# Two MLP weight loads moved ahead of a token load, and a later landing assumed by the scheduler, in a linear-attention plus MLP block

## The chip, the cores and the metric

One core of one Trainium2 chip. The metric is the device time in microseconds of one execution, lower is better. Runs of a single-core program are compared in rounds: the two kernels alternate on the same chip, and a ratio is the mean time of one kernel's fast runs over that of the other's of the same rounds, so it is not quite the ratio of the medians quoted. The granted clock is the share of TensorE's full clock that the chip allowed.

Names used below: TensorE is the matmul engine (PE in the profile, its weight loads PEld), VectorE is DVE, ScalarE is ACT, GpSimd is POOL, SP is the engine whose queue issues nearly all loads here. A load lands when all of its data are there.

## The reference

The block adds three things, for 2048 tokens of width 640, all in bfloat16:

```python
xn = layernorm(x)
# attention, 32 heads of 20: feature maps of q and k are two softmaxes each
q, k, v = split(xn @ wqkv)
phi_q = concat(softmax(q @ w_phi), softmax(-q @ w_phi))      # 40 features per head
phi_k = concat(softmax(k @ w_phi), softmax(-k @ w_phi))
kv, z = sum_s phi_k v, sum_s phi_k
o = (phi_q @ kv) / (phi_q @ z + 1e-6)
# MLP with 1536 hidden columns
h = silu(xn @ w1) * (xn @ w3)
out = x + o @ wo + h @ w2
```

## The kernel before

The program is written as small steps (a matmul group, a softmax, a load), each a stream's next item. At build time a list scheduler estimates when each step could start, takes the earliest, and so fixes the order of instructions on every engine; on the chip each engine runs its list in order and waits on semaphores. The scheduler's estimate of a load:

```python
            if o.dma:
                turn = "T" == o.part                       # a transposing load
                ...
                self.bus = max(self.bus, t + 0.5) + o.cost / rate
                o.end = self.bus + (2.3 if turn and t > 80 else 1.6 if turn else 1.3 if t < 4.5 else 1.9)
```

These constants change no computing instruction and no load. They only move steps in the order (and with it two semaphore instructions of TensorE: 46 in the profile before, 44 after).

The loads that are issued at once, all but one of them from SP, in this order:

```python
    def w13(a, b):                                          # two MLP weights, columns a to b: 640 KB each for 512
        P.dma("SP", w1_s[:, :, a:b], w1_t[:, :, a:b])
        P.dma("SP", w3_s[:, :, a:b], w3_t[:, :, a:b])
    def first_loads():
        ...                                                 # tokens 0-3, wv
        w13(0, 512)
        P.dma("SP", phi_s[:], phi_t)
        P.dma("SP", wqkT[:, DC:2 * DC, :], A_wqkv[:, D:2 * D], True)     # key weights, transposed
        load_x(4, 8)                                        # token tiles 4-7, 640 KB
        load_x(8, 12)
        w13(512, 1024)
```

One MLP step is ten matmuls of 512 columns, five with `w1` and then five with `w3`; steps 0 to 3 use weight columns 0 to 511 and step 4 is the first to need columns 512 to 1023. In the second half, each token tile's query features are computed (`Wqp`), normalised, transposed by a DMA into `EqT`, and used by eleven small matmuls (`KVc,EqT`) that belong to no fixed place in the order: the scheduler fits MLP steps and output tiles between.

```python
    def warm_up():                                          # before the first data has come
        for n, rep in ((4, 8), (1, 7)):                     # 8 matmuls of 512 columns, 7 of 128
            for _ in range(rep):
                mm(bank(7, 128 * n), zero[:], zero[:]..., True, True, ...)
```

The softmax here doesn't subtract the row's maximum and nothing guards it: scores larger than these inputs give would overflow.

Of the kernel before, what the change touches and what calls it, by code (L numbers as in the profile page):

```python
# [45 lines left out]
class _Program:  # L46
# [123 lines left out]
    def commit(self, ops):  # L170
        for o in ops:
            o.idx = len(self.ops)
            o.deps = self.find_deps(o)
            t = self.free[o.eng]
            for d in o.deps:
                t = max(t, d.end + 0.07)
            o.start = t
            if o.dma:
                turn = "T" == o.part
                self.free[o.eng] = t + (max(1.28, o.cost / 120e3) if turn else 0.46)  # L180
                rate = (280e3 if o.cost < 300e3 else 235e3) if turn else 270e3 if t < 2.9 else 330e3 if t < 4.5 else 345e3 if t < 20 else 285e3
                self.bus = max(self.bus, t + 0.5) + o.cost / rate
                o.end = self.bus + (2.3 if turn and t > 80 else 1.6 if turn else 1.3 if t < 4.5 else 1.9)
            else:
                o.end = t + o.cost + LATENCY[o.eng]
                self.free[o.eng] = t + o.cost - OVERLAP[o.eng]
            self.ops.append(o)
            if o.eng == "POOL" and not o.dma:
                self.pool = o
            for g in o.reads:  # L190
                if isinstance(g, tuple):
                    self.bank.setdefault(g, {})[o.eng] = o
                else:
                    self.last_r.setdefault(g, {})[("dma", o.idx) if o.dma else o.eng] = o
            for g in o.writes:
                if isinstance(g, tuple):
                    self.bank.setdefault(g, {})[o.eng] = o
                else:
                    self.last_w[g] = o
                    self.last_r.pop(g, None)  # L200
# [45 lines left out]
def bass_parallel_sum__linear_kernel_hedgehog__glu_gated_swiglu__prompt_kernel(  # L246
# [160 lines left out]
    def w13(a, b):  # L407
        P.dma("SP", w1_s[:, :, a:b], w1_t[:, :, a:b])
        P.dma("SP", w3_s[:, :, a:b], w3_t[:, :, a:b])

    def load_x(a, b):
        P.dma("SP", x_tok[:, a:b, :], x_t[:, a:b, :])

    def first_loads():
        load_x(0, 1)
        o = P.dma("ACT", x_tok[:, 1:2, :], x_t[:, 1:2, :])
        o.reads = P.regions(zero[:])
        load_x(2, 3)
        for a, b in ((0, 2), (2, 4), (4, DC)):
            P.dma("SP", wv[:, a:b, :], wqkv_t[:, a:b, 2 * D:3 * D])  # L420
        load_x(3, 4)
        w13(0, 512)
        P.dma("SP", phi_s[:], phi_t)
        P.dma("SP", wqkT[:, DC:2 * DC, :], A_wqkv[:, D:2 * D], True)
        load_x(4, 8)
        load_x(8, 12)
        w13(512, 1024)


    def consts():  # L430
# [269 lines left out]

    def norms():
        yield lambda: (memset("DVE", zero[:], 0.0), memset("DVE", warm[:], 0.0), first_loads(), consts())
        yield lambda: act_sums(1)
        yield lambda: ln_stats(0, 1)
# [280 lines left out]
```

## Time and profile before

268.77 us, median of three runs (268.58 to 268.81); the profiled execution has a span of 266.6 us.

TensorE is the bound.

The chain of waits of the kernel before, in order of time (start us, length us, what):

```profile
14.78 9.38 DMA w_s<-in_B_w_dram
24.15 0.14 issue
24.29 101.68 PE PS L104 x839
125.97 0.04 issue
126.00 138.34 PE PS L104 x968
```

The chain is TensorE's own work but for two breaks: it starts from a weight load that landed at 24.15 us, and it breaks once more near 126 us. The waits view names the two releasers (us in total, times, longest):

```profile
PEld PS L104 <- DMA EqT<-eqt: 0.4, 1, 0.4
PE PS L104 <- DMA w_s<-in_B_w_dram: 0.4, 1, 0.4
```

TensorE's timeline of the kernel before (start us, us, engine, line, operation, output<-inputs, count, idle before it and its releaser):

```profile
12.76 4.48 PE L104 MATMUL PS<-xnT,w_s 128*128 128x512 bf16 x20
...
22.66 1.24 PE L104 MATMUL PS<-xnT,w_s 128*128 128x512 bf16 x5
24.29 1.24 PE L104 MATMUL PS<-xnT,w_s 128*128 128x512 bf16 x5 [0.39 <-DMA w_s<-in_B_w_dram]
...
27.84 4.24 PE L104 MATMUL PS<-Wkp,xnT 128*128 128x320 bf16 x30
...
122.54 3.42 PE L104 MATMUL PS<-w_s,hT 128*128 128x320 bf16 x24
126.00 0.49 PE L104 MATMUL PS<-KVc,EqT 128*128 128x63 bf16 x11
```

Reading it: matmul ends are modelled, so the 0.39 understates the wait. Five matmuls of 512 columns follow each other every 0.216 us, so the ones that start at 22.66 hand over at 23.74; the next start at 24.29 is 0.55 us late. In the same way the 24 matmuls of 320 columns, 0.136 us apart, that start at 122.54 hand over at 125.80; the start at 126.00 is 0.20 us late. The landings in the trace, in the order of issue: tiles 4-7 at 17.58, tiles 8-11 at 19.37, first weight at 22.43, second weight at 24.16.

### The profile page before, as it was taken

The numbers are of one execution on the slowest core, as the hardware profiler recorded it, in microseconds if no ns is written. First come the engines' busy times: TensorE is split into PE (matmuls) and PEld (weight loads), VectorE is DVE, ScalarE is ACT, GpSimd is POOL, SyncE is SP. The second block draws the span as 40 slices with busy tenths as digits, with TensorE's granted clock in tenths as the row PEclk, the third lists the DMA queues.
The fourth block names the chain that finished last, engine by engine and source line by source line (L and its number), as shares of the span: only waits on it lengthen the run. The fifth ranks groups of instructions, "written<-read, shape, count | busy, mean of one in ns | idle before, by whom it ended". The sixth has DMA issues, their size and how long they took to land.

```text
span 266.6 us, 4819 instructions
## 1 busy us (share of the span) xinstructions
PE 262.1 (98%) x1951; PEld 162.1 (61%) x1951; DVE 182.9 (69%) x312; ACT 107.4 (40%) x227; POOL 95.6 (36%) x107
## 2 busy tenths in 40 slices
PE   7999999999999999999999999999999999999996
PEld 3754666766766756556465655466565746777773
DVE  4567899999777497778767677969775857212112
ACT  5546688898871325332251314451414220000000
POOL 4211289898999032522207030617030430000000
PEclk9999999999999999999999999999999999999999
DMA  7996045962400773619503543061825074331211
GB/s 223 277 316 173 1 105 108 324 85 49 125 0 2 188 247 72 131 28 130 128 0 70 114 85 69 10 128 35 148 52 128 0 126 84 76 98 49 87 38 49
DMA packets 62742, 27.73 MB, mean 104 GB/s; under 512 B 49920, under 2 KB 62720, under 8 KB 62720
## 3 DMA queue, kind: packets, MB, share of 16 engines
q1 hardware_dynamic: 62576, 27.26, 44.4%
q8 instruction: 15, 0.25, 0.4%
q10 hardware_dynamic: 144, 0.16, 0.2%
q14 instruction: 7, 0.06, 0.1%
HBM read 12.81 MB, written 2.62 MB: 58 GB/s over the span
## 4 chain that ended last, share of the span: by engine, by line
PE 90%; SPq 5%; DMA 4%; issue 0%; DVE 0%
PE PS L104 90%; SPq L116 5%; DMA w_s<-in_B_w_dram 4%; DVE xres L104 0%
## 5 line engine op out<-in xcount | busy, mean ns | idle before, releaser
L104 PE MATMUL PS<-xnT,w_s 128*128 128x512 bf16 x480 | 108.6, 379 | 0.4 <-DMA w_s<-in_B_w_dram 0.4
L104 PEld LDWEIGHTS PS<-xnT,w_s 128*128 128x128 bf16 x480 | 46.2, 98 | 51.3 <-DVE Wkp L104 0.9
L104 POOL TENSOR_TENSOR eqt<-eqt,rS 128x600 bf16<-128x600 bf16 (+1 forms) x32 | 41.0, 1304 | 90.8 <-DVE rS L104 90.8
L104 ACT ACTIVATE th<-PS 128x512 f32<-128x512 f32 x48 | 28.6, 595 | 74.0 <-PE PS L104 73.9
L104 PE MATMUL PS<-w_s,hT 128*128 128x320 bf16 (+2 forms) x384 | 54.9, 299 | 0.0
L104 DVE SCALAR_TENSOR_TENSOR t<-th,PS 128x512 bf16<-128x512 f32 x48 | 32.5, 677 | 31.6 <-ACT th L104 31.5
L104 PEld LDWEIGHTS PS<-w_s,hT 128*128 128x128 bf16 x384 | 37.1, 98 | 15.1
L104 POOL TENSOR_TENSOR ekt<-ekt,rS 128x640 bf16<-128x640 bf16 x32 | 39.7, 1273 | 3.9 <-DVE rS L104 3.9
L104 ACT ACTIVATE eqt<-PS 128x240 bf16<-128x240 f32 (+1 forms) x96 | 27.2, 348 | 26.0 <-PE PS L104 24.1
L104 DVE TENSOR_TENSOR xres<-PS,xres 128x640 bf16<-128x640 f32 (+2 forms) x17 | 13.3, 782 | 34.6 <-PE PS L104 34.6
L104 DVE SCALAR_TENSOR_TENSOR hT<-t,PS 128x512 bf16<-128x512 bf16 x48 | 33.0, 687 | 2.0 <-PE PS L104 0.4
L104 ACT ACTIVATE ekt<-PS 128x640 bf16<-128x640 f32 x32 | 22.3, 703 | 7.0 <-PE PS L104 6.4
L104 DVE TENSOR_REDUCE S<-ekt 128x64 f32<-128x1280 bf16 x16 | 23.2, 1452 | 2.2 <-ACT ekt L104 2.2
L104 PE MATMUL PS<-wo_s,oT 128*128 128x320 bf16 (+2 forms) x160 | 24.5, 299 | 0.0
L104 PE MATMUL PS<-wv,xnT 128*128 128x320 bf16 x160 | 24.4, 299 | 0.1
L104 PE MATMUL PS<-Wqp,xnT 128*128 128x360 bf16 (+1 forms) x160 | 24.3, 299 | 0.0
L104 DVE TENSOR_REDUCE S<-eqt 128x66 f32<-128x1320 bf16 x16 | 24.2, 1513 | 0.0
L104 PE MATMUL PS<-Wkp,xnT 128*128 128x320 bf16 x160 | 23.9, 299 | 0.0
L104 PEld LDWEIGHTS PS<-Wqp,xnT 128*128 128x128 bf16 x160 | 15.2, 98 | 7.6
L104 PEld LDWEIGHTS PS<-wv,xnT 128*128 128x128 bf16 x160 | 15.4, 98 | 6.4 <-ACT xnT L104 0.3
L104 PEld LDWEIGHTS PS<-Wkp,xnT 128*128 128x128 bf16 x160 | 15.4, 98 | 6.1
L104 PEld LDWEIGHTS PS<-wo_s,oT 128*128 128x128 bf16 x160 | 15.3, 98 | 6.0
(52 smaller groups left out, 156.7 us busy)
## 6 DMA issues: line engine op xcount, KB each, us to landing
w_s<-in_B_w_dram SPq DMA_DIRECT2D x6, 640.0 KB, 7.2
xres<-in_A_x_dram SPq DMA_DIRECT2D x16, 160.0 KB, 2.5
out_dram<-xres SPq DMA_DIRECT2D x15, 160.0 KB, 1.8
x_tok<-in_A_x_dram SPq DMA_DIRECT2D x3, 640.0 KB, 4.5
w_s<-in_B_w_dram SPq DMA_DIRECT2D x1, 1920.0 KB, 8.8
wo_s<-in_A_wo_dram SPq DMA_DIRECT2D x1, 800.0 KB, 4.7
wv<-in_A_wqkv_dram SPq DMA_DIRECT2D x2, 320.0 KB, 4.3
x_tok<-in_A_x_dram SPq DMA_DIRECT2D x3, 160.0 KB, 2.6
```

The source lines that it names most:

```text
L104: o = _Op(eng, lambda: m(*args, **kw), r, w, cost)
L116: o = _Op(eng, lambda: m(out, in_), self.regions(in_), self.regions(out), nbytes, True)
```

## The change

The intent: bring the weight that TensorE waits for ahead of tokens that are needed 10 us later, and make the scheduler leave more room between the transposing loads of query features and their use.

```diff
-                o.end = self.bus + (2.3 if turn and t > 80 else 1.6 if turn else 1.3 if t < 4.5 else 1.9)
+                o.end = self.bus + (2.7 if turn and t > 80 else 1.6 if turn else 1.3 if t < 4.5 else 1.9)
@@ first_loads
         load_x(4, 8)
+        w13(512, 1024)
         load_x(8, 12)
-        w13(512, 1024)
```

The built programs were compared too. TensorE's order is unchanged up to its matmuls at about 134 us; ACT's and POOL's orders are unchanged throughout.

## The prediction

> **What bounds the kernel now.** TensorE issues without a gap from about 7 us to its end. The page gives PE 98% busy, but matmul ends are modelled, so I used starts: 512-column matmuls follow each other every 0.216 us. The Trainium skill, "TensorE: Matmul & The Clock Gate", "Step-by-step: what each phase is for", gives about 216 ns for N=512; the trace agrees, at a granted clock of 1.00. After 7 us only two places exceed column time by over 0.06 us:
>
> - 24.29 us: 0.55 us (0.4 in the timeline, modelled ends hiding the rest), ended by the second MLP weight load. Landings: token tiles 8-11 19.37, first weight (columns 512-1023) 22.43, second 24.16. The five matmuls before start at 22.66 and need 1.08, so it was due at 23.74.
> - 126.0 us: 0.20 us (0.4 in the waits view), ended by the transposing load of query features of tile 4, which took 5.2 us against a median of 3.7.
>
> The chain of waits agrees: PE 90%, broken at 24.15 and 125.97 alone. Removable from TensorE is therefore about 0.75 us.
>
> **What the change does.**
> 1. Two 640 KB weight loads go ahead of the 640 KB token load on one queue. The skill, "DMA: Bandwidth & Descriptors", "Queues, rings and completion order", says each DMA engine consumes descriptors in ring order; here landings follow issue order. My estimate from those landings: each weight lands 1.8 us sooner, the second near 22.3, 1.4 us before it is due, so the whole 0.55 us goes. The next bound there (the Wkp copy, done at 23.92, for matmuls due after 25.1) isn't met. The tokens land near 24.2; the statistics that read tile 8 start at 34.9, so 10 us of slack remain.
> 2. The assumed landing (2.3 to 2.7) only feeds the scheduler; nothing is added or removed. The built order is unchanged on TensorE up to about 134 us and everywhere on ACT and POOL; TensorE, DVE and SP differ after. The load that now costs 0.20 us is used before that point, behind the same TensorE work, so I expect that wait to stay (0 to 0.4 us). Later loads keep about 0.3 us of slack or more, as before (smallest: 0.26 tile 14, 0.63 tile 11); tile 15 gains some. Worth: 0 ± 0.2 us.
>
> **On the critical path:** all of the 0.55 us. DVE is nearly full (29.3 of 30 us in the 30-60 stretch), but its run of work starts from matmuls that move with TensorE, and so do the later loads. Small slacks near 56 us (transposed tokens 0.39, query weights 0.73) could give back 0.1 if those loads don't move.
>
> **Prediction: 268.2 us** (268.77 - 0.55), 8 in 10 between 267.9 and 268.7. Chances: faster by over 2% 0.01, within 2% 0.98, slower 0.01.
>
> **What would show it.** Right: no PE wait near 24 us; second weight landing near 22.3; the chain no longer through a weight load; about 0.2 us of wait left near 125.5. Wrong for step 1: a weight later than 23.7, or a wait of like size at 56 us. Wrong for step 2: the 125.5 us wait gone, or new waits for query features after 134 us.
>
> **What would make it wrong.** A transposing load that meets other traffic takes 4.7 to 5.2 us (tiles 4, 11, 14) instead of 3.7; in the new order other tiles may be the slow ones, costing up to 1 us each. Or new waits cancel the gain.

## More of the kernel before

The head, part 3 and part 4 of the page of the kernel before: busy time and share by engine, DMA queues (packets, MB, share of 16 engines), and the chain that ended last:

```profile
span 266.6 us, 4819 instructions
PE 262.1 (98%) x1951; PEld 162.1 (61%) x1951; DVE 182.9 (69%) x312; ACT 107.4 (40%) x227; POOL 95.6 (36%) x107
...
q1 hardware_dynamic: 62576, 27.26, 44.4%
q8 instruction: 15, 0.25, 0.4%
...
PE 90%; SPq 5%; DMA 4%; issue 0%; DVE 0%
```

## The result

The changed kernel: 267.92 us median (267.85 to 268.04, six runs), before 268.79 (268.2 to 269.0, six runs); ratio 0.9972, 95% interval 0.9959 to 0.9984. It is correct. By the 2% rule this is "same", with a small gain clear of noise.

The page of the changed kernel:

```profile
span 266.3 us, 4817 instructions
PE 262.7 (99%) x1951; PEld 162.6 (61%) x1951; DVE 182.7 (69%) x312; ACT 107.5 (40%) x227; POOL 95.8 (36%) x107
...
PE 97%; DMA 1%; DVE 1%; POOL 0%; issue 0%; ACT 0%
```

Its chain of waits, from where TensorE takes it over for good:

```profile
10.61 114.99 PE PS L104 x928
125.59 0.03 issue
125.62 138.34 PE PS L104 x968
```

Its waits on loads, and TensorE's timeline at the same places as before:

```profile
PEld PS L104 <- DMA EqT<-eqt: 0.4, 1, 0.4
```

```profile
12.93 4.48 PE L104 MATMUL PS<-xnT,w_s 128*128 128x512 bf16 x20
...
22.82 2.32 PE L104 MATMUL PS<-xnT,w_s 128*128 128x512 bf16 x10
...
27.46 4.24 PE L104 MATMUL PS<-Wkp,xnT 128*128 128x320 bf16 x30
...
122.17 3.42 PE L104 MATMUL PS<-w_s,hT 128*128 128x320 bf16 x24
125.62 0.48 PE L104 MATMUL PS<-KVc,EqT 128*128 128x63 bf16 x11
```

The weight load is out of the chain, the MLP step's ten matmuls run in one piece, and the wait near 126 us is still there (0.19 us by the starts). The landings: first weight 19.53, second weight 22.61, tokens 8-11 24.29. So far this is what was predicted. Two things don't add up, though. The profiled spans differ by 0.4 us only (266.64 and 266.26), since in the changed kernel's profile the first MLP matmul happened to start 0.17 us later; and the timed runs differ by more, 0.87 us by the medians. A wait of 0.55 us read in one execution is not obviously the thing measured.

### The profile page after: what moved, and what is told of

It reads as the page before. It is cut to its first block, busy times and chain, and to the rows that moved or that the text cites. A ratio compares the mean times of both kernels' runs of the same rounds, so it can differ in the third digit from the quotient of the medians.

```text
span 266.3 us, 4817 instructions
## 1 busy us (share of the span) xinstructions
PE 262.7 (99%) x1951; PEld 162.6 (61%) x1951; DVE 182.7 (69%) x312; ACT 107.5 (40%) x227; POOL 95.8 (36%) x107
## 4 chain that ended last, share of the span: by engine, by line
PE 97%; DMA 1%; DVE 1%; POOL 0%; issue 0%; ACT 0%
PE PS L104 97%; DMA x_tok<-in_A_x_dram 1%; DVE bst L104 0%; POOL rstd L104 0%; ACT xnT L104 0%; DVE x_tok L104 0%; DVE xres L104 0%; DVE mv L104 0%
## 5 line engine op out<-in xcount | busy, mean ns | idle before, releaser
L104 ACT ACTIVATE ekt<-PS 128x640 bf16<-128x640 f32 x32 | 22.3, 705 | 6.9 <-PE PS L104 6.4
L104 DVE TENSOR_REDUCE S<-eqt 128x66 f32<-128x1320 bf16 x16 | 24.2, 1514 | 0.1
L104 PE MATMUL PS<-Wkp,xnT 128*128 128x320 bf16 x160 | 23.9, 299 | 0.0
L104 PEld LDWEIGHTS PS<-wv,xnT 128*128 128x128 bf16 x160 | 15.5, 98 | 6.5 <-ACT xnT L104 0.3
```

The lines of the kernel that those rows point to most:

```text
L104: o = _Op(eng, lambda: m(*args, **kw), r, w, cost)
```

## The experiments

Twelve runs, each with five rounds against the kernel before, in three sets of four on three chips. The texts under "expected" use these names:

- Theory A: the second weight's late landing held TensorE for 0.55 us, the load order removes this, and nothing else differs.
- Rival B: a good part of the gain comes from the new order in the second half.
- Theory C, formed after eight runs: both waits are made by TensorE's instruction fetch.

Two measures from the traces serve throughout. The *wait at 24 us* is the start of TensorE's first key-feature matmul (27.84 in the timeline above) minus the start of its first MLP matmul (12.76), minus the 14.52 us of matmuls between them, the figure in every profile without a wait. The *second part* is the time from that key-feature matmul to the start of the last matmul. (Some traces lack the first MLP record; its start is then taken 0.22 us earlier, one matmul.)

### e1: the load order alone

```diff
         load_x(4, 8)
+        w13(512, 1024)
         load_x(8, 12)
-        w13(512, 1024)
```

> Only the load order is changed; the assumed landing stays at 2.3, so every engine but the SP queue has the order of before. Theory A (the second MLP weight load held TensorE for 0.55 us at 24.3 us and nothing else differs): 0.5 to 0.6 us less than before, ratio about 0.998; no wait near 24 us; the second weight lands near 22.5; the wait of about 0.2 us for the query features of tile 4 stays near 125.5, and the slack of tile 14 stays near 0.3 us. Rival B (a good part of the gain, some 0.3 us of the measured 0.75, comes from the new order after 134 us): about 0.45 us less than before and 0.3 us above the changed kernel.

Measured: 268.11 us median against 268.66, ratio 0.9979 (0.9965 to 0.9992). No wait at 24 us; second weight landed at 21.43; the wait for tile 4 stayed (0.26 us, from starts of matmuls). The size is theory A's, but the interval holds B's too.

### e2 and e7: the assumed landing alone, twice

```diff
-                o.end = self.bus + (2.3 if turn and t > 80 else ...
+                o.end = self.bus + (2.7 if turn and t > 80 else ...
```

> Only the assumed landing is changed (2.7); loads as before, the order of TensorE, DVE and SP after 134 us as in the changed kernel. Theory A: same time as before within 0.15 us (ratio 0.9995 to 1.0005), a wait of about 0.55 us at 24.3 us and one of 0.2 us at 126. Rival B: 0.2 to 0.4 us less than before, because small waits that the one profile of before does not show are gone in its other executions.

Measured: 267.97 us against 268.66, ratio 0.9979 (0.9964 to 0.9993). By its time this run speaks for B: it gains as much as e1. Its profile does not: span 266.7 us, close to that of before (266.6), in what was one of its slower runs (268.47 us). So it was repeated on another chip.

> The kernel with the assumed landing alone, once more: its first runs gave 0.56 us less than before, which theory A did not expect, while its profile showed the time of before. Theory A (luck of the first 13 us, which have the same instructions): 268.3 to 268.7 this time, within 0.25 us of before. Rival B (the new order in the second half is worth something that the profiles do not show): again 0.4 to 0.6 us less than before, several runs under 268.1. In the profile: landings of query features by tile as in the other profiles within 0.2 us, a wait of 0.15 to 0.28 us for tile 4.

Measured: 268.25 against 268.58, ratio 0.9996 (0.9977 to 1.0015). The means of the runs differ by 0.53 us in e2 and by 0.06 us in e7. The traces decide better than the times: the second part took 236.23 and 236.36 us in these two, 236.28 to 236.35 in the profiles of before, e4, e1 and e5, which have the old order. By that measure the new order gives nothing.

### e3 and e12: the changed kernel again

> The changed kernel once more, on the chip that the single edits run on. Both theories: ratio to before 0.9972 to 0.9980 (0.55 to 0.75 us less). Theory A: equal to the run with the load order alone within 0.15 us. Rival B: 0.3 us below it.

Measured: 267.99 us against 268.66, ratio 0.9974 (0.9961 to 0.9986); 0.12 us under e1 by the medians, inside the scatter of either (0.5 and 0.7 us).

> The changed kernel a third time, on the same chip as the three others: 267.8 to 268.2, ratio to before 0.997 to 0.998, with a spread of its runs (0.5 us) under that of before (1.2 us).

Measured: 268.04 us against 268.33, ratio 0.9990 (0.9975 to 1.0005): a smaller gain than expected, because before was faster on this chip, and one that is not clear of noise: the interval holds 1. The spread was 0.5 us against 1.2.

### e4: the kernel before again, as a control

> The kernel before under another name, as a control: ratio 1.000 within 0.0005 or so. Its profile shows how constant the wait at 24.3 us (0.55 us) and at 126 us (0.20 us) is from execution to execution. Theory A: both waits are there again, the first between 0.4 and 0.8 us. Rival B: the waits in the second half vary by more than 0.2 us between the two profiles.

Measured: 268.59 us, ratio 0.9997 (0.9981 to 1.0014). Its timeline:

```profile
13.38 4.26 PE L104 MATMUL PS<-xnT,w_s 128*128 128x512 bf16 x19
...
23.06 2.32 PE L104 MATMUL PS<-xnT,w_s 128*128 128x512 bf16 x10
...
27.69 3.56 PE L104 MATMUL PS<-Wkp,xnT 128*128 128x320 bf16 x25
```

The same program, and no wait at 24 us: the second weight landed at 23.70 instead of 24.16, 0.46 us sooner, and TensorE reached the place 0.41 us later, since its first MLP matmul started at 13.17 (the record is missing; 13.38 is the second). So theory A's number was one draw of something that varies. This miss is the most useful line of the set.

### e5: half of the load swap

```diff
         load_x(4, 8)
+        P.dma("SP", w1_s[:, :, 512:1024], w1_t[:, :, 512:1024])
         load_x(8, 12)
-        w13(512, 1024)
+        P.dma("SP", w3_s[:, :, 512:1024], w3_t[:, :, 512:1024])
```

> Half of the load swap: the first MLP weight goes ahead of token tiles 8-11, the second stays behind them; assumed landing 2.3 as before. Theory A (only the landing of the second weight matters, due about 11 us after the first MLP matmul): it lands at 23.7 to 24.2 as before, so nothing is gained: 268.4 to 268.8 and within 0.2 us of before. A theory by which any earlier weight helps would give half of the load swap's gain, 0.3 us.

Measured: 268.47 against 268.58, ratio 1.000 (0.9981 to 1.0018); second weight at 24.19, a wait of 0.73 us. Moving the first weight shows no gain. The interval (0.5 us either way) is too wide to exclude the 0.3 us by itself; the profile speaks against it, with the second weight as late as in the kernel before and TensorE waiting for it.

### e6: more bytes ahead of the weights

```diff
         load_x(8, 12)
+        load_x(12, 16)
         w13(512, 1024)
@@ loads (where tiles 12-15 were loaded before)
-            if t == 7:
-                yield lambda: load_x(12, 16)
```

> The opposite dose: token tiles 12-15 (640 KB more) are also loaded ahead of the two weights. TensorE's order is that of before. Theory A: the second weight lands 1.7 to 1.9 us later, near 25.8, TensorE's first key-feature matmul starts near 29.5 instead of 27.8, and the whole delay stays: 270.3 to 270.7, ratio 1.006 to 1.008. If TensorE had slack to recover later, the time would rise by less than 1 us.

Measured: 270.34 us against 268.58, ratio 1.008 (1.0055 to 1.0105), so 1.8 us by the medians, where 1.7 to 2.1 was expected. Runs from 269.44 to 271.79; the longest had a granted clock of 0.994, and without it the median is 270.18, 1.6 us above before. The profile was of the fastest run: weights at 23.43 and 25.23, the key-feature matmul at 28.92 rather than 29.5, and a wait of 1.52 us:

```profile
23.56 1.24 PE L104 MATMUL PS<-xnT,w_s 128*128 128x512 bf16 x5 [0.63 <-DMA w_s<-in_B_w_dram]
25.36 1.24 PE L104 MATMUL PS<-xnT,w_s 128*128 128x512 bf16 x5 [0.56 <-DMA w_s<-in_B_w_dram]
```

The second part took 236.28 us, the same as before. A delay at 24 us is never made up later: TensorE has no slack behind it.

### What the ten traces had in common by then

All ten traces have packets of 16,384 bytes on the queue that the page calls `q8 instruction`. They come on average every 256 TensorE instructions (counting matmuls, weight loads and the few semaphore instructions between the second and the last one in the trace of before: 3,326 in 13 intervals) and take 0.9 to 1.7 us each. The Trainium skill, "Runtime: NRT & Kernel Launch", "Instruction fetch mechanics", says that an engine's instruction memory is refilled in blocks of 16 KiB, which are 256 instructions, by a DMA queue of the engine's own. This trace agrees. The page, "DMA: Bandwidth & Descriptors", "Queues, rings and completion order", adds that a DMA engine changes queue only between packets; the end packets told below the table fit that.

In the table (worked out from the traces; us), the first such packet comes either near 14 us or near 19 us, and which one it is goes with which load is late. The last four rows are from the third set of runs, made later.

```
run       loads     1st fetch  key wts   1st MLP   2nd weight  wait   tile-4 load    second
                               landed    matmul    landed      at 24  issue to land  part
before    old         18.7      15.01     12.77     24.16      0.55     5.21         236.28
e5        half        18.8      14.89     12.62     24.19      0.73     5.06         236.33
e4        old         14.4      16.65     13.17     23.70      0.01     5.28         236.35
e2        old         14.7      16.95     13.47     24.01      0.01     5.16         236.23
e7        old         14.2      16.36     12.88     23.39      0.00     5.23         236.36
e6        more ahead  14.2      16.40     12.88     25.23      1.52     5.21         236.28
changed   swapped     18.9      15.22     12.94     22.61      0.00     5.19         236.28
e3        swapped     19.0      15.04     12.88     22.54      0.00     5.24         236.31
e1        swapped     13.9      16.05     12.85     21.43      0.01     5.27         236.34
e8        swapped     20.1      15.48     12.71     23.06      0.01     5.29         236.07
e12       swapped     19.7      14.90     12.75     22.69      0.01     5.30         236.38
e11       swapped     19.4      14.93     12.69     22.34      0.00     5.15         236.07
e9        swapped     14.6      16.82     13.04     22.20      0.00     4.38         236.07
e10       old         14.5      16.69     13.24     23.79      0.00     4.72         236.07
```

Fetch near 14: the key weights land at 16.0 to 17.0, and the four loads behind them follow every 1.6 to 1.9 us. Fetch near 19: the key weights land at 14.9 to 15.5, and the third of the four loads comes 2.7 to 3.4 us after the second, whichever load that is. In the old order the third is the first weight and the fourth the second weight, and the wait appears. The fetch is not all that varies: the first MLP matmul starts anywhere from 12.62 to 13.47 us, before the first fetch in every trace, and for a given landing of the second weight an earlier start means a longer wait. The windows of the kernel before show how the end of such a load looks (stretch, length, busy us with counts by engine, granted clock, share of the 16 DMA engines, GB/s):

```profile
21.00:22.00 1.00, 1.00 (x6) 0.44 (x5) 0.84 (x2) 0.84 (x2) 0.55 (x3) 1.00 1.10 348
22.00:22.50 0.50, 0.50 (x11) 0.47 (x10) 0.47 (x2) 0.50 (x1) 0.00 (x0) 1.00 0.60 186
22.50:23.00 0.50, 0.50 (x9) 0.35 (x7) 0.50 (x1) 0.50 (x2) 0.00 (x0) 1.00 0.07 25
23.00:23.50 0.50, 0.50 (x4) 0.20 (x2) 0.50 (x2) 0.50 (x2) 0.00 (x0) 1.00 0.07 23
23.50:24.00 0.50, 0.40 (x2) 0.00 (x0) 0.42 (x1) 0.50 (x2) 0.00 (x0) 1.00 0.18 41
```

348 GB/s until 22 us, and then a whole microsecond at a share of 0.07, about one sixteenth: read as one engine still moving while the other fifteen have nothing left. (The share is summed from packet times and can pass 1.) The skill says why this matters: in "DMA: Bandwidth & Descriptors", "Why a DMA increments its semaphore by 16 and not by 1", the semaphore counts engines that finish independently, so a load has landed only with its last engine. The landing at 24.16, after two windows at 0.07, agrees. (The 0.18 of the last window is a transposing load whose packets start near 23.9.) In e4 the windows from 22.5 to 23.5 show 0.11 and 0.03: a tail too, but a shorter one.

The packets in the traces say it more directly. Each of the four loads ends with 16 packets of 4 bytes, read here as one for each DMA engine. In the kernel before, 15 of those of the second weight come between 22.02 and 22.50 us and the last at 23.68; in e4, 15 come by 22.74 and the last at 23.18. In all seven traces with the fetch near 14 us, the last such packet of the key weights starts within 0.02 us of the fetch's end (15.43 and 15.44 in e4). In all seven with the fetch near 19 us, one engine ends the third load 0.8 to 1.3 us after the other 15, against 0.1 to 0.8 us with the early fetch. This is how one would see a fetch of some 1.1 us hold one DMA engine, with the load in its way waiting for that engine; the traces do not name the engines.

The wait near 126 us has the same look. In the first ten traces a fetch starts at 123.3 to 125.0 us, inside the flight of tile 4's transposing load, which then takes 5.1 to 5.3 us against a median of 3.7 for all sixteen.

### e9 and e10: the instruction fetch moved

If the fetch makes the waits, it should help to move the fetch and nothing else. It comes by instruction count, so the warm-up matmuls were split: the same 4,992 columns in 39 instead of 15 matmuls, 48 more instructions with their weight loads. e9 does this to the changed kernel, e10 to the kernel before. The order of all other instructions stays, as the traces confirm.

```diff
-        for n, rep in ((4, 8), (1, 7)):
+        for n, rep in ((1, 39),):
```

> Theory C, formed from the traces so far: both waits are set by TensorE's instruction fetch, one packet of 16 KB about every 256 TensorE instructions, which holds one of the 16 DMA engines for about 1.1 us, so the load in flight lands late on that engine alone. Here the changed kernel's 8 warm-up matmuls of 512 columns are split into 32 of 128: the same columns, 24 matmuls and 24 weight loads (48 instructions) more ahead of everything. Theory C: the fetch that stood at 123.4 to 124.0 in every profile comes about 4 us earlier, near 119.5; the load of tile 4's query features lands in 3.6 to 4.3 us instead of 5.1 to 5.3 and the wait of 0.2 us near 125.6 is gone; other tiles become the slow ones where a fetch now falls. Time 0 to 0.2 us below the changed kernel. Rival (the load of tile 4 is slow because of the transposing load of output features issued 1.5 us after it): it stays at 5.1 to 5.3 us and the wait stays.

Measured: 267.88 us against 268.33, ratio 0.9984 (0.9968 to 1.0), and 0.16 us below e12 on the same chip by the medians. In its timeline the 24 matmuls hand over to tile 4's on time (122.26 + 3.26 = 125.52):

```profile
122.26 3.42 PE L104 MATMUL PS<-w_s,hT 128*128 128x320 bf16 x24
125.52 0.47 PE L104 MATMUL PS<-KVc,EqT 128*128 128x63 bf16 x11
```

The fetch came at 120.24 instead of 123.4, 3.2 us earlier rather than 4. Tile 4's load took 4.4 us, a little over the 4.3 expected, and landed 0.7 us before its use. No wait is left. The rival explanation, the neighbouring transposing load, falls as the main cause: that load still overlaps it (122.6 to 125.6 us), though it starts 2.1 us after it now and not 1.4. The profiles with the old order settle this better: tile 13's load there has the same neighbours as tile 4's 1.4 and 3.0 us behind it, but no fetch in its way, and takes 3.7 us.

What keeps tile 4's load above the median of 3.7 us is the fetch still, it seems, which now overlaps its start. Over all 14 traces there are 224 loads of query features. Of the 111 with an instruction packet in flight (q8's, or those of 8,192 bytes on q14) 62 took 4.2 us or more; of the 113 without one, the slowest took 4.01 us. The slow loads that the prediction feared, of tiles 11 and 14, are among the 62. So every slow load here had an instruction packet in flight, but not every such packet makes a load slow; why is not shown.

> The same split of the warm-up in the kernel before, load order and assumed landing of before. Theory C: the first fetch comes before 15 us instead of at 14 or 19 us by chance, so the second MLP weight no longer has a straggling engine: it lands at 23.4 to 24.0, with under 0.2 us of wait near 24 us, none near 126; the time falls by 0.2 to 0.6 us to 268.0 to 268.4 with the load order unchanged. Theory A alone (only the load order matters): the time of before, 268.5 to 268.7.

Measured: 267.73 us (267.59 to 268.08) against 268.33, ratio 0.9978 (0.9964 to 0.9993). With the load order and the assumed landing of before, this gains as much as the whole change did, and more than expected. The timeline of e10:

```profile
23.12 2.32 PE L104 MATMUL PS<-xnT,w_s 128*128 128x512 bf16 x10
...
122.46 3.42 PE L104 MATMUL PS<-w_s,hT 128*128 128x320 bf16 x24
125.72 0.47 PE L104 MATMUL PS<-KVc,EqT 128*128 128x63 bf16 x11
```

The MLP step is in one piece, and nothing waits near 126 us. Tile 4's load took 4.72 us here. The last table column agrees to the hundredth: 236.07 us in e9, e10 and in the two runs below whose order leaves more room, and 0.16 to 0.31 more in the ten others. One caution: a first fetch at 14.5 us occurs in the unsplit kernel too (e4), so the one profile of e10 does not prove that the split fixes that fetch. Nor did the split move it: it starts after some 210 matmuls and weight loads in e9 and e10, and less the 48 added ones that is the place of the early fetch in the unsplit kernels (160 to 165; the late one comes after 225 to 239). So the rule by count is shown for the fetch near 123 us and not for the first one. What speaks for a steadier first part is that all five runs stay at or below 268.08, where 5 of the 43 runs of before that were made in all do, and 1 of the 9 on this chip; taking 0.25 us off the 9 for the wait near 126 us (by the last column) would bring 5 of them there.

### e8 and e11: a later landing still

```diff
-                o.end = self.bus + (2.7 if turn and t > 80 else ...
+                o.end = self.bus + (3.0 if turn and t > 80 else ...
```

This is on top of the changed kernel. At 3.0 the scheduler does move the use of tile 4: ten MLP matmuls now stand before it.

> Candidate: load order of the changed kernel, assumed landing 3.0 instead of 2.7. The scheduler now puts ten MLP matmuls (2.16 us) between the slow load of tile 4 and its use, and leaves at least 5.3 us from issue to use for every tile. Theory A: the wait of 0.2 us near 125.6 is gone and no other comes: 0.2 us below the changed kernel, 267.7 to 267.8, ratio to before 0.9965. If other tiles become the slow ones, new waits of 0.1 to 0.5 us appear after 126 us and the time stays at 267.9 to 268.3.

Measured: 267.75 us median against 268.58, but ratio 0.9996 (0.9964 to 1.0027): four runs at 267.59 to 267.86, and two at 269.77 and 269.88. The two long ones had a granted clock of 0.994 where the four had 1.00. An estimate: the fast runs' span of 265.9 us at 0.994 of the clock would be 267.5, so the clock accounts for about 1.6 of the 2.2 us. The ratio mixes the two. In the profile (a fast one, span 265.8 us) no query-feature load is waited for, and the use of tile 4 stands 1.9 us after its landing:

```profile
125.20 2.32 PE L104 MATMUL PS<-xnT,w_s 128*128 128x512 bf16 x10
127.36 0.48 PE L104 MATMUL PS<-KVc,EqT 128*128 128x63 bf16 x11
```

> The candidate with the assumed landing of 3.0 once more, because two of its six runs took 269.8 and the profiled one 267.6. If those two belong to the kernel, at least one of six runs is again over 269 us and a profile of such a run would show a wait of about 2 us. If they were the chip's, all six are 267.5 to 268.0.

Measured: 267.73 against 268.33, ratio 0.9983 (0.9966 to 1.0001); five runs from 267.52 to 268.45, between the two outcomes expected: none over 269, but one over 268.0 by nearly half a microsecond and another by less, all at a granted clock of 1.00. So the long runs of e8 did not come back, and most of their length goes with their lower clock; the other 0.6 us stays unexplained, since no profile caught one. By the profiles (265.8 us twice, against 266.3, 266.2 and 266.2 for the changed kernel) this order is the better one by 0.4 us; by the times it is not shown to beat the changed kernel.

## Why the prediction was right

Predicted 268.2 us, 267.9 to 268.7; measured 267.92, at the low edge.

- **What bounds the kernel.** Right. In every profile TensorE works back to back but for the places named. e6 shows that what is lost at 24 us stays lost.
- **Step 1, the load order.** Right in kind and in detail: second weight near 22.3 predicted, 22.61 measured; tokens near 24.2 predicted, 24.29 measured; no wait left. The term that was wrongly sized is "the whole 0.55 us goes". It was read from one execution. Over five profiles with the second weight behind the tokens (before, e2, e4, e5, e7) the wait is 0.55, 0.01, 0.01, 0.73 and 0.00 us. The timed runs, which are many, show the distribution better: 43 runs of before spread from 267.69 to 269.42 us, 16 runs of the changed kernel from 267.79 to 268.38. The mean falls by 0.56 us (268.56 to 268.00; those runs come from different sets and chips, so this is a rough figure) while the best runs are about equal. What the change removes is the late part of a distribution, not a constant. That 0.55 and 0.56 agree is luck.
- **Step 2, the assumed landing.** Right that it is worth about nothing: the second part averages 236.32 us with the old order (before, e1, e4, e5, e6) and 236.31 with the new one (changed, e2, e3, e7, e12). The wait for tile 4 stayed at 0.15 to 0.30 us, as predicted, because the use of tile 4 lies before the first instruction that moves. Tile 15 gained room as predicted (6.8 us of slack), tiles 11 and 14 too (1.5 and 1.35 us), at the cost of others that had more. In one profile of the old order (e5) tile 14 waited 0.18 us and tile 4 only 0.05; in one of the new order (e7) tile 6 waited 0.05 us. So rival B is not empty, but what was seen of it is under 0.2 us. By times alone it is unsettled: the means of e2 and e7 lie 0.53 and 0.06 us under before (e2's interval is clear of 1, e7's is not), and why e2's timed runs were fast while its profiled one was not is open; a lucky first fetch could do it, but timed runs leave no trace to see it in.
- **Small slacks near 56 us.** They shrank as feared (0.39 to 0.15 and 0.73 to 0.48 us), but cost nothing.
- **Why tile 4's load is slow.** The prediction said "meets other traffic". It does: for tile 4 the traffic that matters is TensorE's own instructions. e9 and e10 show it, and the 224 loads counted above bear it out.
- **The extra 0.2 to 0.3 us.** The medians of the first set differ by 0.87 us; its ratio, 0.9972, means 0.75 us, 0.2 more than predicted. The repeats e3 and e12 gave 0.67 and 0.32 us by the means of their runs. The first set was not special; its interval (0.43 to 1.10 us) holds the predicted 0.55.

What stays open: what decides whether the first fetch comes near 14 or near 19 us, what moves the start of the first MLP matmul, and why the granted clock fell in two runs of e8 and one of e6.

## What to carry to other kernels

When a wait on the bounding engine ends with a load, look at a second execution before sizing it: here the same program showed 0.55 us in one and none in the next, and the gain was in cutting off the late runs. A load whose last microsecond moves at one sixteenth of the DMA engines has a straggler, and a straggler at a fixed place in the program can be the instruction fetch of the busiest engine, which here came by instruction count after the first and was moved by changing that count. And before crediting a scheduler constant, compare the built orders: a constant cannot help a wait that lies ahead of the first instruction it moves.

## What the Trainium skill lacked or had wrong

- "Runtime: NRT & Kernel Launch", "Instruction fetch mechanics", gives the 16 KiB blocks of 256 instructions, which these traces confirm (15 packets of 16,384 bytes), but calls the cost of crossing a block mostly hidden. It lacks that the fetch delays data loads in flight: a load with a fetch in its way lands about 1.2 us late (2.7 to 3.4 us after the one before it instead of 1.8 to 1.9), and tile 4's transposing load took 5.1 to 5.3 us with the fetch, 4.4 and 4.7 us with the fetch moved.
- "DMA: Bandwidth & Descriptors", "Queues, rings and completion order", names row 14 as that of the refill. If the profile numbers its queues as the page does its rows, which no run here shows, that is not the whole of it: the profile has instruction packets on two queues, and the TensorE-paced ones of 16,384 bytes are on q8 (15 packets, 0.25 MB); q14 carries 7 smaller ones (0.06 MB).
- "TensorE: Matmul & The Clock Gate", "Back-to-back issue gap", says that streams of weight-load and matmul pairs sustain about 131 ns per matmul at N=512 and about 81 ns at N=128, and that the formula with about 216 ns over-counts there. Here pairs at N=512 start every 216 ns through the whole kernel, and the eleven pairs of N=63 (one of 42) take 0.32 us together, 29 ns each; pairs at N=128 start 56 ns apart (median of 27 in the trace of before after 7 us). The formula holds, and the sustained figures do not.
- No page has it that the first fetch of one and the same program can come at two places (18.7 us in the profile of before, 14.4 in e4; over all programs here seven profiles near each), with the loads around it timed accordingly.
